# Sixteen words to an entry of the experts' lists, where there were four

## The chip, the cores and the metric

The kernel runs on one core of a Trainium2 chip. The metric is the device time of one execution in microseconds. Three runs of the kernel before were timed.

## The reference

An attention block with a decaying outer-product state makes x, and a top-2 mixture of eight experts works on it.

```python
# attention: B=4, H=8, S=768, D=48
f = sigmoid(f_logit)
for t in range(S):
    state = f[:, :, t, :, None] * state + einsum('bhd,bhe->bhde', k[:, :, t], v[:, :, t])
    y[:, :, t] = einsum('bhd,bhde->bhe', q[:, :, t], state)
x = y.transpose(0, 2, 1, 3).reshape(3072, 384)
# router and experts: E=8, F=1024
noisy = x @ w_gate + log1p(exp(x @ w_noise)) * noise          # (3072, 8)
top2, weights = the two largest of noisy, softmax over the two
for e in range(8):
    for k in range(2):
        m = top2[:, k] == e
        out[m] += weights[m, k, None] * (relu(x[m] @ w1[e]) @ w2[e])
```

## The kernel before, in words

**Attention.** The 3,072 tokens are 24 tiles of 128 (six chunks of the sequence times four batches). Tile n passes seven stages, `forget`, `scaled`, `scores`, `summed`, `output`, `decays`, `features`, and one loop (L1243) issues them for several tiles at once, each stage at its own lag. The inputs f, q, k, v of a tile are four loads of 128 x 8 pieces of 192 bytes, written into rings of 5, 4, 4 and 6 tiles (L424); `load` (L517) puts them on SP's queue in the order of the program, some tiles ahead. `clamp` (L523) works on f, from the second loop step on on POOL. A tile's x goes out to a DRAM table `x_rows` (L631).

**Routing.** After the four tiles of a chunk, `route` (L634) computes the noisy logits, the two experts of each token with their weights, and each token's rank among those of its expert. Its steps are spread over the stages of the next tiles. Its result is `entry` (L475): for each tile and each of the two choices an entry of four words, the row of x, the weight, the token, and a zero. `put` (L700) is one indirect DMA from POOL that writes the 128 entries of a tile and choice to their places in the DRAM table `lists` (L468), where each expert has 3,072 places. There are 48 puts; they are popped one by one between the stages (L1274), and each is followed by a small memset of `spacer`.

**Fill.** Places that no token takes must name a row that exists and a token that is out of bounds. `empty` (L469) holds such entries; four memsets at L1192 write it at the start, and one DMA (L1267, on SP's queue while tile 5 passes `scores`) copies it over all of `lists`. `entry` is cleared and gets its constant words at L1194 to L1196.

**Experts.** An item is a block of 256 places of one expert's list, or two such blocks. `fetch` (L795) loads 256 entries from `lists` into `slots` (SP's queue), `gather` (L806) collects the rows of x by indirect DMA from POOL, `turned` (L822) transposes them into `xt`, and `first_layer` (L872) or `first_of_two` (L891) and `second_layer` (L970) run the two matrix products. The result rows `ys` are scattered with add into `out` (L995). The first items use tokens of the first three chunks alone, so that they begin while attention still runs; further items take blocks of pairs with fewer products, and rests of 32 places go through `fetch_quarter` (L1073) and `quarter_block` (L1092). Behind two flags (L1336) stand code for further rests and a general version; neither is taken here.

**Memory.** SBUF tiles are placed in the order in which the pools and their tiles are made: `top`, `ring`, `moved`, `const`, `rt`, `ffn`, and behind these the attention's working tiles, later replaced by `late`. `empty` and `entry` are in `const`; `xt` and `hs` are in `ffn` and `late`; the expert weights `w1`, `w2` and the gathered rows are in `moved`, ahead of `const`.

The order of instructions on each engine is that of the program from L1199 on (`in_order`). DMAs issued from SP wait there, in order, for their buffers.

Of the kernel before, what the change touches and what calls it, by code (L numbers as in the profile page):

```python
# [12 lines left out]
U32 = mybir.dt.uint32  # L13
# [318 lines left out]
def kernel(  # L332
# [38 lines left out]
    nc = tc.nc  # L371
    B, H, S, D = q.shape
    N, DM = out.shape
    E = moe_w_gate.shape[1]
    FF = moe_w1.shape[2]
    C = 128
    NCH = S // C
# [5 lines left out]
    QS = 32  # L383
# [5 lines left out]
    FAR = 1 << 20  # L389
# [13 lines left out]
    const = ctx.enter_context(tc.tile_pool(name="const", bufs=1))  # L403
# [59 lines left out]
                            pattern=[[1, 128]], channel_multiplier=-1)  # L463


    LR = E * N + 256
    x_rows = tc.dram_tile([N, DM], F32, name="x_rows")
    lists = tc.dram_tile([LR, 4], U32, name="lists")  # L468
    empty = const.tile([128, LR // 128, 4], U32, tag="empty", name="empty")  # L469

    cap = [const.tile([128, HP, C], F32, tag=f"cap{i}", name=f"cap{i}") for i in range(2)]
    for i in range(2):
        nc.gpsimd.memset(cap[i], LCAP)

    entry = const.tile([128, NCH, B, 2, 4], U32, tag="entry", name="entry")  # L475


    XW = 2 * D
# [44 lines left out]
    def clamp(n, engine=nc.gpsimd):  # L523
        if n < NCH * B:
            raw = pads["f"][n % RING["f"]][:, :, 0:D]
            engine.tensor_scalar(raw, raw, XMIN, None, ALU.max)  # L526
# [241 lines left out]
    def value(at, hi):  # L768
        return nc.values_load(at, engines=[mybir.EngineType.SP], min_val=0, max_val=hi,
                              skip_runtime_bounds_check_because="clamped where it is made")  # L770

    slots, xg, xt = {}, {}, {}
# [13 lines left out]
    def item_of(p):  # L786
        return p if p < E else E + (p - E) // 2

    def expert_of(k):
        return k if k < E else NI - 1 - k  # L790
# [4 lines left out]
    def fetch(p):  # L795

        assert len(n_put) >= (HALF if p < E else NCH) * B * 2
        slots[p] = ffn.tile([128, 2, 4], U32, tag=f"slots{p < E}", name=f"slots{p}", bufs=8)
        row = expert_of(item_of(p)) * N + (0 if p < E else 256 * (1 + (p - E) % 2))
        got = nc.sync.dma_start(out=slots[p], in_=lists[row:row + 256, :].rearrange("(s p) w -> p s w", p=128))  # L800
        if p < E:

            tc.declare_no_dep(got.ins, group="later", reason="slots differ")
            tc.add_to_no_dep_group("full", got.ins)
# [265 lines left out]
    slots_q, xg_q = {}, {}  # L1070
    late, w_q = [], []

    def fetch_quarter(n):  # L1073

        slots_q[n] = ffn.tile([128, 4], U32, tag="slots_q", name=f"slots_q{n}", bufs=2)
        row = value(steer_q[n][:, 1:2], E * N)
        for i in range(128 // QS):
            nc.sync.dma_start(out=slots_q[n][i * QS:(i + 1) * QS, :], in_=lists[bass.ds(row, QS), :])

    def gather_quarter(n):  # L1080
        xg_q[n] = late[-1].tile([QS, DM], F32, tag="xg_q", name=f"xg_q{n}", bufs=2)
# [48 lines left out]
    def further(inner, steers):  # L1130

        sb = inner.enter_context(tc.tile_pool(name="sb", bufs=1))
        ps = inner.enter_context(tc.tile_pool(name="ps", bufs=2, space=PSUM))
        same = sb.tile([128, 128], F32, tag="same", name="same")
        make_identity(nc, same)
        for t, (steer, skip, size) in enumerate(steers):
            at, x = sb.tile([128, 4], U32, tag="at", name=f"at{t}"), sb.tile([128, DM], F32, tag="x", name=f"x{t}")
            if size < 128:
                for i, val in enumerate((0, 0, FAR, 0)):
                    nc.vector.memset(at[:, i:i + 1], val)  # L1140
            nc.sync.dma_start(out=at[0:size], in_=lists[skip:][bass.ds(value(steer[:, 1:2], E * N), size), :])
            nc.gpsimd.indirect_dma_start(out=x, out_offset=None, in_=x_rows,
                                         in_offset=bass.IndirectOffsetOnAxis(ap=at[:, 0:1], axis=0))
            e = value(steer[:, 0:1], E - 1)
            w1, w2 = sb.tile([128, KO, FF], F32, tag="w1", name=f"w1{t}"), sb.tile([128, FO, DM], F32, tag="w2", name=f"w2{t}")
            nc.sync.dma_start(out=w1, in_=moe_w1[bass.ds(e, 1)].rearrange("o (k p) f -> p (o k) f", p=128))
            nc.sync.dma_start(out=w2, in_=moe_w2[bass.ds(e, 1)].rearrange("o (f p) d -> p (o f) d", p=128))
            p = ps.tile([128, 512], F32, tag="p", name=f"px{t}")
            for i in range(KO):
                nc.tensor.transpose(p[:, i * 128:(i + 1) * 128], x[:, i * 128:(i + 1) * 128], same)  # L1150
            turn = sb.tile([128, KO, 128], F32, tag="turn", name=f"turn{t}")
            nc.vector.tensor_copy(turn.rearrange("d k t -> d (k t)"), p[:, 0:DM])
            h = sb.tile([128, FO, 128], F32, tag="h", name=f"h{t}")
            for fo in range(FO):
                p = ps.tile([128, 512], F32, tag="p", name=f"ph{t}_{fo}")
                for i in range(KO):
                    nc.tensor.matmul(p[:, 0:128], lhsT=w1[:, i, fo * 128:(fo + 1) * 128], rhs=turn[:, i, :],
                                     start=(i == 0), stop=(i == KO - 1))
                nc.scalar.activation(h[:, fo, :], p[:, 0:128], AF.Relu)
            p = ps.tile([128, 512], F32, tag="p", name=f"py{t}")  # L1160
            for fo in range(FO):
                nc.tensor.matmul(p[:, 0:DM], lhsT=h[:, fo, :], rhs=w2[:, fo, :], start=(fo == 0), stop=(fo == FO - 1))
            y = sb.tile([128, DM], F32, tag="y", name=f"yf{t}")
            nc.vector.tensor_scalar(y, p[:, 0:DM], at[:, 1:2].bitcast(F32), None, ALU.mult)
            nc.gpsimd.indirect_dma_start(out=out, out_offset=bass.IndirectOffsetOnAxis(ap=at[:, 2:3], axis=0),
                                         in_=y, in_offset=None, bounds_check=N - 1, oob_is_err=False, compute_op=ALU.add)
# [22 lines left out]
        nc.vector.tensor_tensor(rest, more, bad, ALU.max)  # L1189

    zero = moved.tile([128, DM], F32, tag="zero", name="zero", bufs=1)
    for i, val in enumerate((0, 0, FAR, 0)):  # L1192
        nc.gpsimd.memset(empty[:, :, i], val)
    nc.gpsimd.memset(entry, 0)  # L1194
    for i, ids in ((0, row_of), (2, token)):
        nc.gpsimd.tensor_copy(entry[:, :, :, :, i], ids.unsqueeze(3).broadcast_to((128, NCH, B, 2)))  # L1196
# [46 lines left out]
    for i in range(-3, NS + 2):  # L1243
        for stage, lag in ((forget, -3), (scaled, -1), (scores, 0), (summed, -2), (output, 1), (decays, -2), (features, 2)):
            n = i - lag
            if not 0 <= n < NS:
                continue
            stage(n)
            if stage is forget:
                load("f", n + 4)  # L1250
                clamp(n + 2, nc.gpsimd if n else nc.vector)
            elif stage is scaled:
                for nm in "qk":
                    load(nm, n + 2) if n < 4 else load(nm, n + 3)
                    if n == 3:
                        load(nm, n + 3)
                if n < 2:
                    load_router(n)
                while xw:
                    xw.pop(0)()  # L1260
            elif stage is scores:
                for m in (n + 1,) if n < 4 else (2 * n - 3, 2 * n - 2) if n < 6 else (n + 3,):
                    load("v", m)
                if n in (2, 6, 7, 8, 9, 10):
                    load_router(2 + (2, 6, 7, 8, 9, 10).index(n))
                elif n == 5:
                    nc.sync.dma_start(out=lists.rearrange("(p r) w -> p r w", p=128), in_=empty)  # L1267
            elif stage is output:
                if 5 <= n < 5 + NS // 2:
                    zeros(1)  # L1270
            next(router, None)
            slot += 1
            if puts and (slot % 3 == 0 or n_routed >= HALF):
                puts.pop(0)()  # L1274
            next(first_pairs, None)

            if done["turned"] and (n_first < 5 or i >= NS - 3 and stage is not forget) and (n_first < 11 or i >= NS - 1):
                next(pieces)
                n_first += 1
        if i < 0:  # L1280
            warm_up(4)
        if i >= NS - 1:
            while xw:
                xw.pop(0)()
        n = i - 2
        if n >= 0 and n % B == B - 1:
            c = n // B
            router = chain(router, route(c))
            n_routed = c + 1
            if c == HALF - 1:  # L1290
                router = chain(router, enough())
                first_pairs = first_loads()
            if c == NCH - 1:
                router = chain(router, plan(), beyond())
# [16 lines left out]
    for item, piece in pieces:  # L1311
        p = item if item < E else 2 * item - E + (piece >= 15)
# [4 lines left out]
        n = item - E - 2  # L1317
# [52 lines left out]
```

## Time and profile before

| | |
|---|---|
| median of three timed runs | 663.89 us (662.24 to 664.91) |
| profiled execution, its own time | 658.81 us |
| its span | 656.5 us |
| TensorE busy | 640.0 us, 97% |
| VectorE, ScalarE, POOL busy | 445.2, 249.7, 269.2 us |
| DMA | 108.90 MB, mean 166 GB/s, 157,161 packets |

The span is the profiled stretch of one execution; the own time has what lies around it. PE is TensorE, PEld its weight loads, DVE VectorE, ACT ScalarE, POOL GpSimd, SP SyncE, which here issues DMAs; SPq is SP's queue. L702 is line 702 of the kernel. A group's line gives the line, the engine, the operation, the tile written and those read, a count and durations. A wait's line names the engine that waited, its tile and line, and behind the arrow what it waited for; then microseconds in total, times, and the longest. "DMA share" is the mean busy share of the core's 16 DMA engines.

### The profile page before, as it was taken

To read this page: it belongs to the slowest core of one execution; us is meant where nothing else is said; L and a number is where in the kernel's file an instruction comes from. 1 tells how busy PE (TensorE), PEld (TensorE's weight loads), DVE (VectorE), ACT (ScalarE), POOL (GpSimd) and SP (SyncE) were. 2 spreads that over 40 slices of the span, in tenths; PEclk is the share of its full clock that TensorE was granted. 3 is DMA by queue.
4 is the path that set the end of the run, shared out by engine and by line. 5 is a ranking of instruction groups with operands and counts; after the bars stand their busy time and mean duration, and the time that the engine had idled before them with its cause. 6 is when DMAs were issued, how large, how long until landed. Compare 5 with 4: busy or idle time off the path is not lost.

```text
span 656.5 us, 13307 instructions
## 1 busy us (share of the span) xinstructions
PE 640.0 (97%) x5075; PEld 586.6 (89%) x5075; DVE 445.2 (68%) x1017; ACT 249.7 (38%) x611; POOL 269.2 (41%) x300
## 2 busy tenths in 40 slices
PE   8999999999999999999999999999999999999991
PEld 8999999888999999999999998998989989889891
DVE  7777878884667445544777767776676777766751
ACT  5876876743221221222333423333233333332320
POOL 7734899828476333212405033150341513413021
PEclk9999999999999999999999999999999999999997
DMA  9999997898799856532325485672954738602122
GB/s 178 183 220 200 205 196 126 179 299 286 225 216 257 263 171 205 174 103 49 73 97 119 121 270 163 228 203 72 303 169 166 211 110 306 183 2 25 22 25 29
DMA packets 157161, 108.90 MB, mean 166 GB/s; under 512 B 115536, under 2 KB 147280, under 8 KB 157088
## 3 DMA queue, kind: packets, MB, share of 16 engines
q1 hardware_dynamic: 144912, 88.70, 49.1%
q0 software_dynamic: 12176, 19.25, 14.0%
q8 instruction: 42, 0.69, 0.5%
q14 instruction: 31, 0.25, 0.1%
HBM read 88.56 MB, written 19.62 MB: 165 GB/s over the span
## 4 chain that ended last, share of the span: by engine, by line
PE 85%; POOL 8%; DVE 2%; DMA 2%; issue 1%; ACT 0%; POOLq 0%; DVEq 0%
PE y L986 32%; PE hp L878 13%; PE P L905 7%; PE Z L905 4%; PE V L905 4%; PE X L905 4%; PE W L905 4%; POOL lists L702 4%; PE xgp L827 2%; PE y L590 2%; PE xp L625 2%; PE sc L572 2%; POOL f_all L526 2%; PE yp_q L1120 1%; PE hp_q L1105 1%
## 5 line engine op out<-in xcount | busy, mean ns | idle before, releaser
L995 POOL DMA_INDIRECT out_dram<-ys,slots x48 | 80.4, 1675 | 198.3 <-ACT ys L1052 169.7
L986 PE MATMUL y<-qk_all,f_all 128*128 128x192 f32 x576 | 105.3, 326 | 0.0
L986 PEld LDWEIGHTS y<-qk_all,f_all 128*128 128x128 f32 x576 | 93.6, 190 | 0.2 <-DVE f_all L968 0.2
L878 PE MATMUL hp<-xt,w 128*128 128x256 f32 x384 | 86.2, 381 | 0.0
L878 PEld LDWEIGHTS hp<-xt,w 128*128 128x128 f32 x384 | 72.0, 190 | 9.6 <-issue 0.3
L986 PE MATMUL y<-w,hs 128*128 128x192 f32 x384 | 70.8, 327 | 0.0
L986 PEld LDWEIGHTS y<-w,hs 128*128 128x128 f32 x384 | 63.7, 190 | 1.2
L968 DVE TENSOR_TENSOR f_all<-hs 128x512 f32<-128x512 f32 x48 | 32.4, 689 | 41.9 <-ACT hs L880 36.5
L810 POOL DMA_INDIRECT xg<-x_rows,slots x48 | 50.2, 1046 | 25.9 <-DMA slots<-lists 11.9
L702 POOL DMA_INDIRECT lists<-entry,sloti x48 | 54.8, 1142 | 9.9 <-issue 9.3
L880 ACT ACTIVATE hs<-hp 128x512 f32<-128x512 f32 x32 | 19.1, 597 | 70.7 <-PE hp L878 70.7
L1126 POOL DMA_INDIRECT out_dram<-ys_q,slots_q x5 | 8.6, 1715 | 80.4 <-DVE ys_q L1124 80.4
L1052 ACT ACTIVATE ys<-ys,slots 128x384 f32<-128x384 f32 x24 | 14.8, 615 | 66.6 <-DVE ys L1051 64.7
L905 PE MATMUL P<-sides,v_all 128*128 128x256 f32 x128 | 38.1, 379 | 0.0
L828 ACT COPY xt<-xgp 128x384 f32<-128x384 f32 x32 | 15.3, 477 | 56.7 <-PE xgp L827 56.7
L941 ACT ACTIVATE hs<-hs 128x256 f32<-128x256 f32 x32 | 13.4, 418 | 59.4 <-DVE hs L921 59.4
L986 PE MATMUL y<-qk_all,hs 128*128 128x192 f32 x192 | 35.1, 326 | 0.0
L986 PE MATMUL y<-w,f_all 128*128 128x192 f32 x192 | 35.1, 326 | 0.0
L575 DVE TENSOR_TENSOR A<-sc,causal 128x1024 f32<-128x1024 f32 x24 | 29.3, 1221 | 7.7 <-PE sc L572 7.4
L905 PE MATMUL X<-xt,w 128*128 128x256 f32 x128 | 32.9, 379 | 0.0
L905 PE MATMUL Z<-xt,v_all 128*128 128x256 f32 x128 | 32.9, 379 | 0.0
L1044 DVE TENSOR_TENSOR ys<-P,y 128x192 f32<-128x192 f32 x24 | 8.5, 354 | 34.6 <-PE y L986 19.8
(189 smaller groups left out, 1385.8 us busy)
## 6 DMA issues: line engine op xcount, KB each, us to landing
w<-in_moe_w_dram SPq DMA_DIRECT2D x28, 1536.0 KB
w_q<-in_moe_w_dram SPq DMA_DIRECT2D x10, 1536.0 KB
f_all<-in_f_logit_dram SPq DMA_DIRECT2D x24, 192.0 KB
qk_all<-in_q_dram SPq DMA_DIRECT2D x24, 192.0 KB
qk_all<-in_k_dram SPq DMA_DIRECT2D x24, 192.0 KB
v_all<-in_v_dram SPq DMA_DIRECT2D x24, 192.0 KB
x_rows<-xs SPq DMA_DIRECT2D x24, 192.0 KB
out_dram<-zero SPq DMA_DIRECT2D x24, 192.0 KB
```

The source lines that it names most:

```text
L575: nc.vector.tensor_tensor(A[n].rearrange("j r (a i) -> j (r a) i", i=C), sc.rearrange("j r (a i) -> j (r a) i", i=C), causal.unsqueeze(1). ...
L702: into = nc.gpsimd.indirect_dma_start(out=lists, out_offset=bass.IndirectOffsetOnAxis(ap=sloti[:, r, b:b + 1], axis=0), in_=entry[:, c, b, ...
L810: nc.gpsimd.indirect_dma_start(out=xg[p][:, s, :], out_offset=None, in_=x_rows[0:HALF * B * C] if p < E else x_rows, in_offset=bass.Indire ...
L828: (nc.vector.tensor_copy if p < E else nc.scalar.copy)(xt[p][:, :, s * 128:(s + 1) * 128], xp[:, 0:DM].rearrange("d (k t) -> d k t", k=KO))
L878: nc.tensor.matmul(hp[:, o, :], lhsT=w1[home(k)][:, i, (fo + o) * 128:(fo + o + 1) * 128], rhs=xt[k][:, i, :], start=(i == 0), stop=(i == ...
L880: nc.scalar.activation(hs[:, fo:fo + 2, :], hp, AF.Relu)
L905: nc.tensor.matmul(to, lhsT=x, rhs=y, start=start, stop=stop)
L941: nc.scalar.activation(c(1, 1), c(1, 1), AF.Relu)
L968: nc.vector.tensor_tensor(sm[which], x, y, op)
L986: nc.tensor.matmul(P[name], lhsT=x[:, o, :], rhs=y[:, o, :], start=(o == 0), stop=(o == FH - 1))
L995: into = nc.gpsimd.indirect_dma_start(out=out, out_offset=bass.IndirectOffsetOnAxis(ap=slots[p][:, s, 2:3], axis=0), in_=ys[s], in_offset= ...
L1052: nc.scalar.mul(ys[1], ys[1], gate[1])
```

## The change

An entry has 16 words in `lists` and in `entry` instead of four; the twelve words behind the first four are zero and are never read. A put writes all 16. The readers take the first four words of each row. `lists` has 25,088 rows instead of 24,832. `empty` holds a quarter of the rows and is written by two memsets, one over all of it and one over the token word; four DMAs copy it, two while tile 3 passes `scores`, one at tile 4 and one at tile 5.

```diff
-    LR = E * N + 256
+    LR = E * N + 512
+    LW = 16
     x_rows = tc.dram_tile([N, DM], F32, name="x_rows")
-    lists = tc.dram_tile([LR, 4], U32, name="lists")
-    empty = const.tile([128, LR // 128, 4], U32, tag="empty", name="empty")
+    lists = tc.dram_tile([LR, LW], U32, name="lists")
+    empty = const.tile([128, LR // 128 // 4, LW], U32, tag="empty", name="empty")
...
-    entry = const.tile([128, NCH, B, 2, 4], U32, tag="entry", name="entry")
+    entry = const.tile([128, NCH, B, 2, LW], U32, tag="entry", name="entry")
...
-        got = nc.sync.dma_start(out=slots[p], in_=lists[row:row + 256, :].rearrange("(s p) w -> p s w", p=128))
+        got = nc.sync.dma_start(out=slots[p], in_=lists[row:row + 256, 0:4].rearrange("(s p) w -> p s w", p=128))
...
-            nc.sync.dma_start(out=slots_q[n][i * QS:(i + 1) * QS, :], in_=lists[bass.ds(row, QS), :])
+            nc.sync.dma_start(out=slots_q[n][i * QS:(i + 1) * QS, :], in_=lists[bass.ds(row, QS), 0:4])
...
-    for i, val in enumerate((0, 0, FAR, 0)):
-        nc.gpsimd.memset(empty[:, :, i], val)
+    nc.gpsimd.memset(empty, 0)
+    nc.gpsimd.memset(empty[:, :, 2], FAR)
     nc.gpsimd.memset(entry, 0)
...
-                elif n == 5:
-                    nc.sync.dma_start(out=lists.rearrange("(p r) w -> p r w", p=128), in_=empty)
+                elif 3 <= n < 6:
+                    for m in (0, 1) if n == 3 else (n - 2,):
+                        nc.sync.dma_start(out=lists.rearrange("(g p r) w -> g p r w", g=4, p=128)[m], in_=empty)
```

More of the change, by code (lines that the diff above doesn't have):

```diff
@@ L1140, in further @@
                     nc.vector.memset(at[:, i:i + 1], val)
-            nc.sync.dma_start(out=at[0:size], in_=lists[skip:][bass.ds(value(steer[:, 1:2], E * N), size), :])
+            nc.sync.dma_start(out=at[0:size], in_=lists[skip:][bass.ds(value(steer[:, 1:2], E * N), size), 0:4])
             nc.gpsimd.indirect_dma_start(out=x, out_offset=None, in_=x_rows,
```

## The prediction

> **What bounds the kernel now.** I read the page first, then the busy time by stretches, then the waits of TensorE, then the list's own groups, and last the packets and the start.
>
> ```profile
> span 656.5 us, 13307 instructions
> PE 640.0 (97%) x5075; PEld 586.6 (89%) x5075; DVE 445.2 (68%) x1017; ACT 249.7 (38%) x611; POOL 269.2 (41%) x300
> PE 85%; POOL 8%; DVE 2%; DMA 2%; issue 1%; ACT 0%; POOLq 0%; DVEq 0%
> ```
>
> TensorE has 640.0 of 656.5 us. Of the chain that ended last 85% is TensorE; the 8% on POOL are mostly stretches in which TensorE was busy too. So what matters is where the other 16.5 us are. The stretches tell (us from:to; busy us of PE, PEld, DVE, ACT, POOL with counts; granted clock; DMA share; GB/s):
>
> ```profile
> 0.00:66.00 66.00, 63.77 (x808) 58.70 (x808) 50.12 (x99) 47.67 (x120) 36.10 (x65) 1.00 0.94 196
> 66.00:130.00 64.00, 64.00 (x917) 58.24 (x917) 53.01 (x134) 46.12 (x126) 57.98 (x78) 1.00 0.87 178
> 130.00:150.00 20.00, 19.17 (x248) 16.37 (x246) 16.46 (x36) 9.62 (x27) 6.77 (x8) 1.00 0.98 285
> 150.00:216.00 66.00, 66.00 (x416) 61.32 (x411) 39.51 (x121) 15.90 (x35) 43.57 (x61) 1.00 0.90 246
> 216.00:643.00 427.00, 427.00 (x2701) 392.00 (x2699) 285.70 (x629) 130.39 (x306) 122.25 (x90) 1.00 0.51 146
> 643.00:656.50 13.50, 0.03 (x1) 0.00 (x0) 0.42 (x1) 0.00 (x0) 2.50 (x2) 0.66 0.28 34
> ```
>
> TensorE is idle 2.23 us up to 66, nearly all before the first tile is through, 0.83 us at the hand-over from attention to experts (130 to 150), and 13.47 us at the end, where the last scatters and the flags run. The change touches nothing after 643. It can win at most the 0.83 us and some tenths of the start; for more, runs without the profiler must hold stalls that this one lacks. TensorE's waits are all of it:
>
> ```profile
> PE warm L1207 <- DVE ones L435: 1.1, 1, 1.1
> PE fp L532 <- DVE f_all L526: 0.7, 1, 0.7
> PE xgp L827 <- ACT yT L605: 0.7, 1, 0.7
> PE qp L532 <- DMA qk_all<-in_q_dram: 0.2, 1, 0.2
> ```
>
> **What the lists cost now.** From the group of the lists:
>
> ```profile
> L702 POOL DMA_INDIRECT lists<-entry,sloti x48: 954/990/1931, 68.3 to 209.1; - x48
> L1267 SPq DMA_DIRECT2D lists<-empty x1: 920/920/920, 45.5 to 45.5; - x1
> DMA to landing us min/median/max: 4.9/6.5/10.4
> ```
>
> A put costs POOL 0.99 us for 128 rows of 16 bytes; a gather of 128 rows of 1,536 bytes has a median of 1.01 us (the group of xg). POOL's price does not follow the bytes: four times the bytes, no change. The packet records show a put as 16 packets of 128 bytes at 15 ns (median): 768 packets, 0.7 us spread over 16 engines. But other packets get stuck beside them: in slices of 4 us the longest 192-byte load packet is 0.2 to 0.9 us from 20 to 68, before the puts, and 2.0, 1.4 and 1.8 us in the three slices from 100 to 112, where the median is still 15 ns. DMA falls behind there:
>
> ```profile
> 66.00:96.00 30.00, 30.00 (x443) 27.45 (x441) 23.64 (x57) 22.35 (x62) 26.98 (x36) 1.00 0.92 197
> 96.00:116.00 20.00, 20.00 (x288) 18.25 (x281) 17.47 (x46) 14.16 (x38) 18.37 (x25) 1.00 0.77 139
> ```
>
> Counting packets in the order of issue (1,024 of 192 bytes to a load), a load of q, k or f mostly drains in 0.9 to 1.4 us before the puts (at most 2.0), and in 2.0 to 2.7 us from 97 to 111. The lead of a k tile over its transpose falls from 10.3 us at tile 16 to 3.85 us at tile 20 and is 5.6 at tile 23. It never reaches zero, so TensorE pays nothing. Whole 64-byte writes may cure this; the cure meets no wait of TensorE.
>
> **The change part by part.**
>
> Start, on POOL. Out go four memsets of 194 strided words (468 ns each, 1.87 us) and one of 192 words (0.31): 2.18. In come memsets of 784 and 768 words and one of 49 strided words. From the 128-word memset (204 ns) to the 512-word one (514 ns) a word costs 0.81 ns: 0.73 + 0.72; at the dearer rate of the 192-word one (1.62 ns a word) 1.27 + 1.25. The small one lies between 0.13 (32 words) and 0.47. In all 1.58 to 2.99 us, so -0.6 to +0.8; I take -0.2, as the flat memset of 448 words (461 ns) lies on the cheap rate. Behind them POOL waits 0.88 us for the tile of its first clamp at 8.41, which hides either end. The one leak is DVE: its first clamp, beside busy POOL, takes 1.05 us, its third, with POOL idle, 0.36. A clamp more or less under a memset is +0.7 or -0.7; I take 0.
>
> The fill, on SP's queue and DMA. One fill of 388 KB was 128 packets of 3,104 bytes at 122 ns: 1.04 us of 16 engines, drained in 1.5 us. Now there are four of 392 KiB: 3.1 us of DMA work more, 4.6 at the drained pace, and three more issues of some 0.9 us on SP. Two stand ahead of f tile 11, one ahead of f tile 12, the last where the old one was. Queued behind them on SP are the loads, the stores of x_rows and the noise. The leads: v tile 5 lands at 40.7 and is used at 45.1, 4.4 us, against two fills (2.1 to 3.1): 1.3 left. f tiles 11 to 14 have 6.2 to 7.2 over their clamps, against 3.1 to 4.6: 1.6 left. q and k have 9.4 and more. Four loads (1,024 packets of 15 ns on 16 engines, 0.96 us) and two stores (128 of 65 ns, 0.52 us) need 4.9 us of DMA in each 6.0 us step, so the lag is worked off at about 1.1 us a step, before the puts begin at 68. Nothing on TensorE: 0. If the cover were gone, each us of lag is a us.
>
> The puts. A packet of 512 bytes lies between the 192-byte one (15 ns) and the 1,536-byte one (65): 27 ns, 0.6 us of DMA more in all. The two ends: puts that stick the others no longer (the 0.83 us of the hand-over go), or twice as much (the 3.85 us lead is gone and TensorE waits some 2 us). The first gathers drain at 143.5 and TensorE starts on them at 143.69, so that stretch is tight. I take -0.4, half of the idle time: the long packets stand beside the puts, which speaks for the first end, but the wait at 143.69 is put down to ScalarE, not to the gather.
>
> [...] The stuck packets show a stall, not its cause; no row separates 16 from 64 bytes.
>
> The reads. `slots` and `slots_q` still fetch 16 bytes a row, now 64 apart: the trace's 6,784 packets of 16 bytes at 9 ns stay. The fetch at 218.10 that waited 3.1 us for the last put is followed on SP by a weight load at 225.22 that waits for TensorE. 0.
>
> SBUF. `empty` grows by 32 bytes a partition and `entry` by 2,304: all tiles made later (route, expert inputs, hidden rows, attention work) move by 2,336 bytes, 36.5 times 64. Rows on this: `sloti` and `slot` are 32-byte tiles in two copies 32 bytes apart, and their six casts take 171 to 179 ns; the eight `slots` copies are 32 bytes apart and the 24 scalings at L1034 take 454 to 456. So 0 by the nearest rows, but these are small operands on other engines than TensorE.
>
> Sum: 658.8 (656.5 span and 2.3 around it) - 0.4 = 658.4. The median of the timed runs, 663.9, lies 5.1 above the profiled execution; with the same gap that is 663.5.
>
> **The rivals.**
>
> Faster, 659: the runs of 662.2 to 664.9 are 3.4 to 6.1 us longer than the profiled one. If that is TensorE waiting for loads or first gathers, at leads of 3.9 and 0.2 us, whole writes give it back: 663.9 - 5 = 658.9. For it: the stuck packets, the tight hand-over. Against: this trace shows no such wait, and the gap may lie outside of the kernel's waits.
>
> Slower, 671, by layout: 1,088 matmul passes read `xt` or `sides` as moving operand (384 at L878, 704 at L905), now off a 64-byte line. If each costs one more read of 8 words at its own pace (12 passes of 256 words in 2.59 us, 216 ns each, so 6.7 ns), that is 7.3 us: 671.2. It decides if reads do not run ahead; half of it is still slower by 0.5%. Against: the casts and scalings above.
>
> Slower, 668, by the fills: if four fills cost more than the 4.4 us lead (say 2.2 us each, as loads did among puts), v tile 5 and the f tiles come late and the stalls, up to 4 us, are not regained, as TensorE has no idle time to give.
>
> That whole lines are not what unsticks the engines is the forecast with its -0.4 left out: 663.9.
>
> **How the numbers follow.** No change that counts 0.45, faster by freed DMA 0.25, layout 0.18, fills 0.12. About 0.5% (3.3 us) is what a measurement of this kernel can tell from none: faster 0.25, same 0.45, slower 0.30. Likeliest 663.5, its own range 661.5 to 665.5. The 8-in-10 range reaches to the rivals' prices: 658.5 to 671.0.
>
> **What would show it.** TensorE near 640 us busy and packed from 15 to 643; v tile 5 landed before 45 us; DMA share above 0.85 between 96 and 116 with no 192-byte packet over 1 us if whole writes unstick the engines; L878 at 381 ns and L986 at 326 if layout is nothing. A wait of TensorE on a load between 32 and 70 us, or longer matmuls at L878, would prove me wrong.

## The result, and the profile after

The first comparison put the changed kernel at 671.40 us (four runs, 667.83 to 673.57) and the kernel before at 663.21 (four runs, 662.24 to 664.91): ratio 1.0115, 95% interval 1.0066 to 1.0165. The prediction was 663.5 with a range up to 671.0, so this is 7.9 us slower than predicted and above the top of the range. (Times are medians; a ratio and its interval come from the single runs and need not be the ratio of the medians. Five runs of before that lie over 1.5% above its fastest on their occasion are left out of the ratios: 1,266, 1,342 and 3,770 us beside the second timing of after, 673.27 us beside the fifth, and 680.42 us beside the last timing of pitch only.) The same kernel, timed again on other occasions (an occasion is the runs of one comparison, taken on one chip one after the other), was no slower than before: 658.36 against 658.67, 658.49 against 658.81, 657.85 against 658.70. On a further occasion it was slower again: 670.69 against 663.81, ratio 1.0106 (1.0055 to 1.0157). What follows is about both halves of that: why the change is worth nothing where the machine is undisturbed, and what is known of the other occasions, on which before itself needs 662 us and more.

The page of the profiled execution after (671.40 us), whose span and busy times answer to those of before:

```profile
span 669.3 us, 13308 instructions
...
PE 645.6 (96%) x5075; PEld 589.7 (88%) x5075; DVE 442.3 (66%) x1017; ACT 250.0 (37%) x611; POOL 262.3 (39%) x298
...
PEclk9999999997999999999999999999999999999996
```

TensorE is busy 5.6 us longer and idle 7.2 us longer (669.3 - 645.6 = 23.7, before 16.5). One slice of the clock row reads 7: the granted clock fell to a half for 6.8 us from 153.7 us on. The same stretches as before (from:to; length, then busy us of PE, PEld, DVE, ACT, POOL; clock; DMA share; GB/s):

```profile
0.00:66.00 66.00, 63.78 (x804) 58.74 (x804) 49.33 (x98) 47.30 (x118) 35.81 (x63) 1.00 0.96 207
66.00:130.00 64.00, 62.77 (x876) 55.99 (x870) 48.23 (x128) 44.82 (x120) 52.09 (x76) 1.00 0.87 199
130.00:150.00 20.00, 19.57 (x270) 16.95 (x265) 14.92 (x28) 9.83 (x28) 12.89 (x17) 1.00 0.88 276
150.00:216.00 66.00, 59.83 (x372) 54.07 (x371) 35.89 (x112) 15.23 (x34) 27.51 (x39) 0.95 0.66 212
216.00:655.00 439.00, 438.95 (x2771) 403.54 (x2771) 293.50 (x653) 132.75 (x311) 130.90 (x104) 1.00 0.51 146
```

TensorE is idle no longer than before up to 66 us (63.78 busy against 63.77), where the four fills run, and not after 216. All the new idle time but that of the end (13.6 us against 13.5) lies between: 1.23 us idle from 66 to 130, where before had none, and 6.17 from 150 to 216. The waits of TensorE say what for:

```profile
PE hp L879 <- issue: 6.0, 1, 6.0
...
PE sc L573 <- issue: 0.8, 4, 0.2
```

"issue" is a wait that this view puts down to nothing: no load, no gather, no other engine. (The timelines say more about the 6.0 us; they are read under "What the occasion does".) The put is as cheap as expected, 48 at 0.98 us (median; before 0.99). The issues of the four fills took SP 1.35 us (median) where 0.9 was expected, and 0.96 and 1.09 in the second and third profile of after:

```profile
L703 POOL DMA_INDIRECT lists<-entry,sloti x48: 954/982/2002, 68.9 to 223.6; - x48
...
L1269 SPq DMA_DIRECT2D lists<-empty x4: 1009/1348/1594, 33.7 to 48.0; - x4
```

### The profile page after: what moved, and what is told of

It reads as the page before. It is cut to its first block, busy times and chain, and to the rows that moved or that the text cites. A ratio compares the mean times of both kernels' runs of the same rounds, so it can differ in the third digit from the quotient of the medians.

```text
span 669.3 us, 13308 instructions
## 1 busy us (share of the span) xinstructions
PE 645.6 (96%) x5075; PEld 589.7 (88%) x5075; DVE 442.3 (66%) x1017; ACT 250.0 (37%) x611; POOL 262.3 (39%) x298
## 4 chain that ended last, share of the span: by engine, by line
PE 93%; issue 2%; DVE 1%; DMA 1%; ACT 1%; POOL 0%; POOLq 0%; DVEq 0%
PE y L987 31%; PE hp L879 13%; PE P L906 6%; PE Z L906 4%; PE V L906 4%; PE X L906 4%; PE W L906 4%; PE sc L573 4%; PE xp L626 4%; PE y L591 4%; PE xgp L828 2%; PE y L602 2%; PE fp L533 2%; PE qp L533 2%; PE ds L597 1%
## 5 line engine op out<-in xcount | busy, mean ns | idle before, releaser
L987 PE MATMUL y<-qk_all,f_all 128*128 128x192 f32 x576 | 105.2, 326 | 0.0
L879 PE MATMUL hp<-xt,w 128*128 128x256 f32 x384 | 87.9, 386 | 6.1 <-issue 6.0
L987 PEld LDWEIGHTS y<-qk_all,f_all 128*128 128x128 f32 x576 | 93.6, 190 | 0.2 <-DVE f_all L969 0.2
L879 PEld LDWEIGHTS hp<-xt,w 128*128 128x128 f32 x384 | 73.2, 193 | 16.5 <-issue 6.6
L987 PE MATMUL y<-w,hs 128*128 128x192 f32 x384 | 70.8, 327 | 0.0
L987 PEld LDWEIGHTS y<-w,hs 128*128 128x128 f32 x384 | 63.7, 190 | 1.2
L811 POOL DMA_INDIRECT xg<-x_rows,slots x48 | 50.6, 1055 | 17.9 <-issue 10.4
L703 POOL DMA_INDIRECT lists<-entry,sloti x48 | 51.8, 1079 | 9.9 <-issue 9.6
L906 PE MATMUL P<-sides,v_all 128*128 128x256 f32 x128 | 38.1, 379 | 0.0
L987 PE MATMUL y<-qk_all,hs 128*128 128x192 f32 x192 | 35.1, 326 | 0.0
L987 PE MATMUL y<-w,f_all 128*128 128x192 f32 x192 | 35.1, 326 | 0.0
L906 PE MATMUL X<-xt,w 128*128 128x256 f32 x128 | 32.8, 379 | 0.0
L906 PE MATMUL Z<-xt,v_all 128*128 128x256 f32 x128 | 32.8, 379 | 0.0
```

What stands on the lines that cost most here:

```text
L703: into = nc.gpsimd.indirect_dma_start(out=lists, out_offset=bass.IndirectOffsetOnAxis(ap=sloti[:, r, b:b + 1], axis=0), in_=entry[:, c, b, ...
L811: nc.gpsimd.indirect_dma_start(out=xg[p][:, s, :], out_offset=None, in_=x_rows[0:HALF * B * C] if p < E else x_rows, in_offset=bass.Indire ...
L879: nc.tensor.matmul(hp[:, o, :], lhsT=w1[home(k)][:, i, (fo + o) * 128:(fo + o + 1) * 128], rhs=xt[k][:, i, :], start=(i == 0), stop=(i == ...
L906: nc.tensor.matmul(to, lhsT=x, rhs=y, start=start, stop=stop)
L987: nc.tensor.matmul(P[name], lhsT=x[:, o, :], rhs=y[:, o, :], start=(o == 0), stop=(o == FH - 1))
```

## The experiments

Two theories at first: one of the parts (whole writes, fills, layout) costs some 8 us, or none does and the first comparison met something else. Four kernels put the parts one by one.

Pitch only: a put writes 16 bytes at a pitch of 64.

```diff
-        nc.vector.tensor_copy(sloti, slot)
+        nc.vector.tensor_scalar(sloti, slot, float(LW // 4), None, ALU.mult)
...
-                out=lists, out_offset=bass.IndirectOffsetOnAxis(ap=sloti[:, r, b:b + 1], axis=0),
-                in_=entry[:, c, b, r, :], in_offset=None)
+                out=lists.rearrange("l (a w) -> (l a) w", w=4), out_offset=bass.IndirectOffsetOnAxis(ap=sloti[:, r, b:b + 1], axis=0),
+                in_=entry[:, c, b, r, 0:4], in_offset=None)
```

> After, but a put writes only the first 16 bytes of its 64-byte row; rows, fills and layout stay as in after. Theory 'whole writes' (the 64-byte writes themselves, or the loads that they let run ahead, cause the 10 us lost between 98 and 161 us): 663 to 665 us, the longest 192-byte packets between 96 and 116 us back near 2 us, the wait of TensorE before the first hp matmuls under 1 us. Rival 'fills': 671. Rival 'layout': 671.

Small fill:

```diff
-                elif 3 <= n < 6:
-                    for m in (0, 1) if n == 3 else (n - 2,):
-                        nc.sync.dma_start(out=lists.rearrange("(g p r) w -> g p r w", g=4, p=128)[m], in_=empty)
+                elif n == 5:
+                    for e in range(E):
+                        nc.sync.dma_start(out=lists[e * N + 512:e * N + 1024, :].rearrange("(p r) w -> p r w", p=16), in_=empty[16 * e:16 * e + 16, 0:32])
+                    nc.sync.dma_start(out=lists[E * N:LR, :].rearrange("(p r) w -> p r w", p=128), in_=empty[:, 0:4])
```

> After, with one fill of 288 KB (the rows 512 to 1023 of each expert and the 512 of the tail, in nine transfers at step 5) in place of four of 392 KB; the rows that no block reads are not filled. Theory 'whole writes': 671 us, the wait of some 6 us before the first hp matmuls stays. Rival 'fills' (three more transfers shift the loads): 663 to 665. Rival 'layout': 671.

Before with room, and before with three unused fills:

```diff
     entry = const.tile([128, NCH, B, 2, 4], U32, tag="entry", name="entry")
+    const.tile([128, 584], U32, tag="room", name="room")
```

> Before, with an unused tile of 2,336 bytes a partition behind the entries: every later tile lies where it lies in after. Theory 'whole writes': 663 to 665 us. Rival 'layout': 671, with a wait before the first hp matmuls. Rival 'fills': 663 to 665.

```diff
+    dummy = tc.dram_tile([3, 128, 784], U32, name="dummy")
+    full = const.tile([128, 784], U32, tag="full", name="full")
...
-                elif n == 5:
-                    nc.sync.dma_start(out=lists.rearrange("(p r) w -> p r w", p=128), in_=empty)
+                elif 3 <= n < 6:
+                    for m in (0, 1) if n == 3 else (n - 2,):
+                        if m < 3:
+                            nc.sync.dma_start(out=dummy[m], in_=full)
+                        else:
+                            nc.sync.dma_start(out=lists.rearrange("(p r) w -> p r w", p=128), in_=empty)
```

> Before, with three transfers of 392 KB from an unused tile to an unused tensor where after has its three more fills. Theory 'whole writes': 663 to 665 us. Rival 'fills': 670 to 672, with a wait before the first hp matmuls. Rival 'layout': this kernel moves tiles by 3,136 bytes, 49 lines of 64 bytes, so 663 to 665 by it.

Measured, beside a before of 658.58 us (31 runs): 658.49 (ratio 0.9997, 0.9984 to 1.0009), 657.91 (0.9991, 0.998 to 1.0001), 658.18 (1.0002, 0.999 to 1.0013) and 658.38 (1.0002, 0.9993 to 1.0012). No part costs 0.2% here. (Pitch only was also expected to bring the long packets back; its longest 192-byte packet took 0.65 us, which is taken up below.) But before is also 4.6 us faster than in the first comparison, so the parts had not yet been tried under the condition in which the whole lost. The whole was, next.

> After, unchanged, timed anew. Pitch-only puts, the small fill, the layout and the dummy fills each ran within 0.1% of before (658.6 us there). Theory 'interaction' (whole writes and four fills cost only together): 668 to 672 us while before is at 658 to 659, with some 6 us of TensorE wait before the first hp matmuls. Rival 'occasion' (the first comparison, where before itself ran at 662 to 665 us, met a disturbance that neither kernel makes, and after only had less margin against it): 658 to 659 us beside a before of 658.6, TensorE's completion events never more than 2.9 us apart before 230 us, and the first hp matmuls at 146 to 147 us; or, where before runs at 662 to 665 again, after above it again.

> Pitch-only puts again, beside after on the same chip. Theory 'interaction': 658 to 659 us, at least 1.5% under after. Rival 'occasion': the same as after where before is at 658.6; where before runs at 662 to 665, both above before, by up to 8 us.

After 658.36 and pitch only 658.18 beside a before of 658.67 (ratios 1.0004, 0.9995 to 1.0013, and 0.9993, 0.9982 to 1.0004). The theory of an interaction falls: parts and whole are alike, and none differs from before by 0.2%. The same program thus has spans of 656.0 and 669.3 us. So the occasion decides, and the question splits: does the change do anything, and what does the occasion do?

**What the change does.** The prediction left open whether whole writes free the loads that stick beside puts. The next runs asked what it is in the rows that frees them, and whether that is worth time once DMA is pressed.

> After, unchanged, a third time (the second time it ran at 658.4 beside a before of 658.7). Theory 'occasion': 658 to 659 us and ratio 0.998 to 1.002 where before is at 658 to 659; only where before itself is at 662 or above, 668 or more. Rival 'real loss of 1%': 665 us or more beside a before of 658.7.

> After with entries of 32 bytes in place of 64 (two fills in place of four). Theory 'pitch' (the nearer the rows of concurrent puts lie, the longer other packets stick beside them): the longest 192-byte packet lies between the 0.65 to 0.85 us of the 64-byte kernels and the 1.2 to 1.3 us of those with 16; the sum of all 192-byte packets between 95.7 and 97.8 us. Rival 'only whole 64-byte lines are clean': 1.2 us and 97.8 again. Time by both: 658 to 659 us.

After ran at 658.49 against 658.81 (0.9991, 0.998 to 1.0002), entries of 32 bytes at 658.56 (1.0003, 0.9991 to 1.0014). From the packet records, over all profiles of each kind without extra copies (long: 192-byte load packets of over 0.6 us that start between 66 and 212 us, while the puts run; sum: the packet time of all 98,304 load packets over 16 engines; the last column is over the whole run):

| rows of the lists | kernels | long | sum, us | longest weight packet (4,096 bytes), us |
|---|---|---|---|---|
| pitch 16, write 16 | before (two profiles), room, unused fills (two) | 14 to 42 | 97.6 to 101.4 | 1.9 to 3.0 |
| pitch 32, write 32 | entries of 32 bytes | 1 | 95.1 | 1.2 |
| pitch 64, write 16 | pitch only (four) | 0 to 4 | 95.4 to 95.6 | 1.1 to 1.4 |
| pitch 64, write 64 | after (five), small fill | 0 to 2 | 95.1 to 96.1 | 1.1 to 1.4 |

Writing all 64 bytes is not what frees the loads: 16 bytes written at a pitch of 64 do it as well (0 to 4 long packets), and so do 32 at 32 (one). Of the pitches tried only 16 bytes makes other packets stick (14 to 42). That it would go by degrees, with 95.7 to 97.8 us for rows of 32 bytes, did not come true: 95.1 is as clean as 64. The table does not show the cause.

Is it worth time? The same ten extra copies went into before and into after:

```diff
...
                 if 5 <= n < 5 + NS // 2:
                     zeros(1)
+                if 12 <= n < 22:
+                    nc.sync.dma_start(out=extra[n - 12], in_=moe_w1[0, 0:96, :])
```

> Before, with one extra copy of 384 KB from DRAM to DRAM on SP's queue in each of the ten steps 12 to 21 (some 2.1 us of 16 engines each, beside 4.9 us of loads and stores in a step of 6.0). Theory 'headroom' (the 64-byte pitch lets the loads run ahead, which is worth time only where DMA is the bound): the lead of 3.85 us is eaten, TensorE waits for loads, 661 to 668 us. Rival 'dense DMA itself delays TensorE's completions': 665 us or more, with completion events more than 3 us apart. If DMA has more to give than that: 658.6.

> After, with the same ten copies. Theory 'headroom': the lead of 15 us at tile 20 covers the copies, 658 to 660 us, 2 to 8 us under before with the copies. Rival 'dense DMA itself delays completions': as slow as before with the copies, or slower.

Before goes to 661.17 us (1.0052, 1.0026 to 1.0077, against 658.81), after stays at 658.53 (0.9994, 0.9984 to 1.0003). A copy took 1.2 us of 16 engines, less than expected. The waits of TensorE from start to end, first of before with the copies, then of after with them:

```profile
PE xgp L828 <- DMA xg<-x_rows,slots: 1.4, 1, 1.4
PE warm L1208 <- DVE ones L435: 1.1, 1, 1.1
```

```profile
PE warm L1209 <- DVE ones L435: 1.1, 1, 1.1
PE fp L534 <- DVE f_all L528: 1.0, 1, 1.0
```

In after the third longest is 0.3 us, and none is for DMA. In before the copies come out as 1.4 us of waiting for the first gather at the hand-over; the smallest lead of a k tile (tiles 14 to 23) is 4.3 us there, 9.1 in after. The single runs of before with the copies spread from 659.07 to 666.01 us, and the profiled one took 660.53. So the changed rows buy headroom of DMA, and without extra traffic there is nobody to spend it. That it is their pitch is argued from the table; pitch only did not run with the copies. The lead alone does not tell the kernels apart: at tile 20 it is 9.0 us in one profile of pitch only. The same pair from one chip, with no copies:

> Before itself, profiled beside its own timed runs: the null of the comparison, and a profile from the same chip as the next run. 658 to 659 us, ratio within 0.2% of 1, if this chip is like the last three. Theory 'pitch' (16-byte rows make other packets stick, 32 and 64-byte rows don't): the longest 192-byte packet 1.2 us or more, all of them 97.8 to 101 us of packet time. Rival 'the stuck packets of the first profile belonged to that occasion': under 0.9 us and 96. If the chip is one where before needs 662 to 665: a wait or late completion events near the hand-over at 140 to 150 us.

> After beside it. Theory 'occasion': the same as before within 0.2% where before runs at 658 to 659; 5 to 9 us above it where before runs at 662 to 665. Rival 'real loss': 665 us or more either way. The longest 192-byte packet under 1.1 us, 95 to 96 us in all.

Before against itself: 658.92 to 658.70 (0.9998, 0.9985 to 1.0011). After: 657.85 (0.9987, 0.9978 to 0.9997), the only one of the twelve undisturbed intervals without copies that leaves 1 out, by 0.03%; one in twelve at 95% is little more than chance gives. Before again has 14 long packets, the longest 1.9 us, so they belong to the kernel and not to the first profile's occasion. The DMA rows from 96 to 116 us, before again and then after:

```profile
96.00:116.00 20.00, 20.00 (x302) 18.14 (x298) 18.07 (x47) 13.41 (x35) 18.20 (x26) 1.00 0.92 194
...
130.00:150.00 20.00, 18.80 (x240) 16.14 (x239) 17.66 (x36) 9.55 (x26) 11.29 (x16) 1.00 0.94 295
```

```profile
96.00:116.00 20.00, 20.00 (x293) 18.20 (x290) 17.77 (x46) 13.84 (x37) 18.34 (x25) 1.00 0.95 223
...
130.00:150.00 20.00, 19.84 (x258) 16.92 (x260) 17.27 (x37) 10.04 (x27) 13.82 (x19) 1.00 1.06 366
```

At nearly the same share of DMA time, 223 GB/s come through instead of 194. Divided by the share, this stretch has 181 to 212 GB/s in the five profiles with rows 16 bytes apart and 227 to 235 in the eight undisturbed ones with rows 32 or 64 apart, none of them with copies. TensorE is full from 96 to 116 either way; at the hand-over it is idle 0.16 us instead of 1.20. With rows 16 bytes apart that number varies (0.83 in the first profile, 1.49 with room, 0.16 and 0.63 with unused fills); in the other eight it is 0.15 to 0.17.

**What the occasion does.** Then an occasion like the first came up, for after alone and for both kernels with the copies doubled:

```diff
-                    nc.sync.dma_start(out=extra[n - 12], in_=moe_w1[0, 0:96, :])
+                    for m in (0, 1):
+                        nc.sync.dma_start(out=extra[2 * (n - 12) + m], in_=moe_w1[m, 0:96, :])
```

> After, unchanged, beside another set of runs of before. Theory 'occasion': 657.5 to 659 us and 0.1% at most from before. Rival 'real loss': 665 us or more.

> Before with two extra copies of 384 KB in each of the ten steps 12 to 21. One copy took 1.2 us of 16 engines, so a step of 6.0 us now needs 4.9 + 2.4 = 7.3, and ten steps fall 13 us behind against leads of 8 to 13 us. Theory 'headroom': TensorE waits for loads or for the first gathers, 662 to 672 us. If the copies only fill DMA's idle time after the loads: 661 as with one copy.

> After with the same copies. Theory 'headroom': leads of 10 to 16 us cover most of it, 658 to 663 us, at least 2 us under before with the same copies. Rival 'after has less margin at the hand-over': above before with the same copies, TensorE waiting before the first hp matmuls.

Beside a before of 663.81 us: after 670.69 (1.0106, 1.0055 to 1.0157), before with two copies a step 687.78 (1.0373, 1.0301 to 1.0445), after with them 670.44 (1.0094, 1.0063 to 1.0126). Both kernels with copies took longer than expected (662 to 672, and 658 to 663 us). On this occasion after alone is 6.9 us slower than before; with the copies the order turns round, and the changed kernel is 17.3 us faster. TensorE's longest waits, first of before and then of after with double copies:

```profile
PE qp L533 <- DMA qk_all<-in_q_dram: 6.7, 5, 2.4
PE xgp L828 <- DMA xg<-x_rows,slots: 4.2, 1, 4.2
PE kp L533 <- DMA qk_all<-in_k_dram: 3.3, 4, 1.4
```

```profile
PE xgp L829 <- DMA xg<-x_rows,slots: 2.3, 1, 2.3
PE y L592 <- issue: 1.7, 2, 1.1
```

And copies of 22 us of 16 engines leave the time of after where it was on that occasion (670.44 against 670.69), so a denser DMA by itself does not make its loss larger. What it loses is seen when two of the five profiles of after are laid side by side, the third (undisturbed) and the fifth (disturbed). The third:

```profile
150.00:165.00 15.00, 15.00 (x124) 13.17 (x121) 4.43 (x16) 4.32 (x11) 4.17 (x8) 1.00 0.55 192
```

and the fifth:

```profile
150.00:165.00 15.00, 12.42 (x63) 8.84 (x64) 3.57 (x9) 1.63 (x4) 6.36 (x12) 0.77 0.57 202
```

From 150 to 165 us half as many matmuls start. The timeline of TensorE (start, us, engine, line, count, and in brackets the idle time before it) shows how, in the third run and then in the fifth:

```profile
150.11 0.67 PE L602 MATMUL y<-qP,st 64*64 64x128 f32 x16
150.71 1.56 PE L879 MATMUL hp<-xt,w 128*128 128x256 f32 x6
```

```profile
153.75 0.45 PE L602 MATMUL y<-qP,st 64*64 64x128 f32 x8
154.43 0.31 PE L602 MATMUL y<-qP,st 64*64 64x128 f32 x1 [0.23 <-issue]
155.15 0.27 PE L602 MATMUL y<-qP,st 64*64 64x128 f32 x1 [0.41 <-issue]
155.86 0.42 PE L602 MATMUL y<-qP,st 64*64 64x128 f32 x2 [0.44 <-issue]
157.28 1.07 PE L602 MATMUL y<-qP,st 64*64 64x128 f32 x3 [1.00 <-issue]
158.72 0.44 PE L602 MATMUL y<-qP,st 64*64 64x128 f32 x1 [0.37 <-issue]
```

Sixteen matmuls of one product, with no wait for another engine or a load in the trace, start within 0.67 us in the one and take 5.4 us in the other, the late ones at steps of 0.71 us or twice that. From 157.4 us on, before the product is through, the granted clock is a half for 6.8 us. Of the 11.5 us between the two spans 3.6 are lost before 150 us, 4.8 in this product, 2.5 in the hp passes behind it, which run at half clock, and 0.6 later.

In the first run of after the 6.0 us look different. From its timelines of TensorE and VectorE:

```profile
148.95 0.49 PE L828 MATMUL xgp<-ident,xg 128*128 128x128 f32 x3
156.46 0.56 DVE L829 COPY xt<-xgp 128x384 f32<-128x384 f32 x1 [0.58 <-remote]
157.08 4.11 PE L879 MATMUL hp<-xt,w 128*128 128x256 f32 x10 [6.02 <-issue]
```

("remote" stands for a releaser that the profile does not name.) The matmuls of hp read xt, and they start 0.06 us behind the copy that makes it. So here TensorE did wait for another engine. The copy in turn began 7.0 us after the product xgp that it reads was done; in the third run the same two steps are 0.4 us apart, with DVE still busy in between. What DVE waits for is the increment of a semaphore by which TensorE reports. From 147.7 to 151.1 us six products end whose increments come 2.2, 3.0, 3.9, 5.9, 7.0 and 7.0 us later (in the third run 0.02 us), and in each case the copy or operation on ScalarE or VectorE that waits for it starts 0.02 to 0.03 us behind the increment. The ends of matmuls are modelled in these profiles, so it stays open whether the matmuls or their reports were late. The increments come 0.75, 1.42, 2.86, 1.43 and 1.58 us apart, near multiples of the 0.71 us of the fifth run.

Both runs of after on such occasions show this from 75 to 225 us, and in the same stretch their traces miss records: 1,797 and 1,822 increments of the semaphores, against 3,027 to 3,129 in the other three. Every profile of an undisturbed occasion has 8,541 to 8,729 of these records in all, the first profile of before among them (8,557), every one of the disturbed ones 6,968 to 7,614, the kernels with double copies at the upper end.

The lost records and the pauses fall in the same 150 us; no run here shows that the one makes the other, and before itself was never profiled on such an occasion. One explanation, code that reaches TensorE late, finds no support: from 75 to 225 us the third and the fifth run each have 19 packets in the queues that the page calls instruction, with a median of 0.93 and 0.95 us.

Which part of the change loses more on such an occasion? Pitch only and unused fills once more:

> Pitch-only puts (16 bytes at a pitch of 64, four fills). On a chip where before needs 658 to 659 us: the same within 0.2%. On one where before needs 662 to 665: 669 to 672 if the pitch or the fills (loads and transfers bunched earlier) make the loss there, 662 to 665 if the 64-byte writes do.

> Before with three unused fills. On a chip where before needs 658 to 659 us: the same within 0.2%. On one where before needs 662 to 665: 669 to 672 if the fills or the shift of the tiles make the loss there, 662 to 666 if the puts' rows do, by their pitch or their bytes.

An undisturbed occasion: 658.05 and 658.87 against 658.61 (0.9985, 0.997 to 1.0001, and 0.9998, 0.9983 to 1.0014); it repeats the null and tells nothing of the others. And again:

> Pitch-only puts (16 bytes at a pitch of 64, four fills). On a chip where before needs 658 to 659 us: the same within 0.2%. On one where before needs 662 to 665: 669 to 672 if the pitch or the fills make the loss there, 662 to 665 if the 64-byte writes do.

This one was disturbed, more than the others: before 668.98 us (665.65 to 680.42), pitch only 674.61, ratio 1.0067 (1.0025 to 1.0109). It is the same program that had 658.05 an occasion earlier. Its timeline has the same picture at another product:

```profile
155.38 0.81 PE L573 MATMUL sc<-qP,kQ 64*128 64x128 f32 x4 [0.45 <-issue]
156.79 0.82 PE L573 MATMUL sc<-qP,kQ 64*128 64x128 f32 x4 [0.60 <-issue]
158.22 0.59 PE L573 MATMUL sc<-qP,kQ 64*128 64x128 f32 x2 [0.61 <-issue]
```

So the extra loss does not need 64-byte writes; it comes with 16 bytes at a pitch of 64, four fills and the moved tiles too. Pitch, fills and layout were not told apart under this condition: the runs meant for it met undisturbed occasions. The extra loss on disturbed occasions is measured (two intervals for after, one for pitch only, all above 1); its cause is open. The granted clock goes with it: beside the fifth run all four runs of after have a mean of 0.987 or 0.988, and 12 of the 13 of before 0.990 to 0.993; the one run of before at 0.987 took 673.27 us.

## Why the prediction was wrong, and where it was right

The step that failed is the last line of the sum: "with the same gap that is 663.5". The sum itself, 658.8 - 0.4 = 658.4, is what after takes on undisturbed occasions (658.36, 658.49, 657.85). The gap of 5.1 us between the profiled execution and the median was taken as a constant that any version would carry. In the comparison the gap was zero: the profiled execution of after took 671.40 us, which is also the median, and that is 13.0 above the sum. The gap of before was the mark of a disturbed occasion: by its complete records and its 658.81 us the profile of before came from an undisturbed execution, by their times the timed runs did not. What such an occasion adds is no constant either: from one kind of occasion to the other before took 5.2 us more (658.6 to 663.8), after 12.3 (658.4 to 670.7), and pitch only 16.6 (658.05 to 674.61, on the worst occasion, where before took 10.4 more). What the runs show in place of the gap is TensorE's pauses, late reports and half clock of the last section, which the prediction had nowhere. Before itself was not profiled there, and why after loses more than before stays open. The rival "faster" was the only place where the gap was looked at; it read it as waits for loads that freed DMA would return, and the sign was the opposite.

By its own steps, the rest:

- *What bounds the kernel.* Right: TensorE, busy for 97% of the span before and 96% in the first profile of after. (The list of its waits leaves out a fifth, 0.2 us for VectorE at L575.) Loads cost it little: none in the first, third, fourth and fifth profile, and in the second 0.6 and 0.4 us near 15 us and 0.5 us at 45. On an undisturbed occasion after has the hand-over at 19.84 of 20 us busy.
- *Start.* The three memsets took 0.74, 0.18 and 0.74 us, 1.66 in all, near the low end of 1.58 to 2.99. The leak by DVE is real: the first f transposes start at 5.10 us instead of 4.79 in every kernel with the changed memsets. The times do not show it.
- *The fill, 0.* Right in the time, with a thinner cover than reckoned. The 1.3 us that were to be left of the lead of v tile 5 were 1.9 to 4.3 us in four profiles of after (from the last landing to the use; by this measure before had 3.7). In the second profile, an undisturbed one, the last landing came at 45.16 us, and TensorE, which started on the tile at 45.30, had waited for it:

```profile
PE y L591 <- DMA v_all<-in_v_dram: 0.5, 1, 0.5
```

  Two experiments on fills lie within 0.1% of nothing, and that comparison has 658.36 against 658.67. The rival at 668 falls.
- *The puts, -0.4.* The packets of 512 bytes took 27 ns, as worked out. The stuck packets went, the k lead of after at tile 20 is 11.0 to 15.9 us, and the difference to before is -0.3, -0.3 and -0.9 us in the three undisturbed comparisons. That agrees with -0.4, but two of the three intervals do not tell it from 0, and 0.4 us was below what a measurement here can show. The reason is a neighbour of the stated one: the pitch frees the loads (0 to 4 long packets at 64, whether 16 or 64 bytes are written), not the write of all 64 bytes. What the trace of before did not tell is that its lead of 3.85 us was a low one; the other kernels with 16-byte rows and no copies have 7.6 to 11.4 there.
- *Layout, 0.* Right. L987 took 326 ns, L906 379, L879 381 on undisturbed occasions, as before, so the 6.7 ns a pass, the author's estimate, show nowhere, and the tile of 2,336 bytes alone gives 1.0002. The rival at 671 had the right number by the wrong way: in the first run L879 rose from 381 to 386 ns, through passes at half clock, 384 x 5 ns = 1.9 us, and the others of the experts kept their times.
- *What would prove it wrong.* Both signs that were named appeared in some profile, and neither is the failure. The wait for a load, 0.5 us at v tile 5, came in an undisturbed run; the longer matmuls at L879, 386 and 389 ns, came from the half clock (in the first run 631 ns a pass there, 379 behind it). The failure came by what was not named: TensorE's pauses and late reports on some occasions.

## What to carry to other kernels

If a profiled execution is some us faster than the timed runs, the gap is a term to be explained, not a constant to be added: take a second profile, on the occasion of the timed runs, before the medians are compared. Time the same program on several occasions before a difference of 1% is put down to an edit; here one program gave 658 and 675 us, and each comparison's interval held only for its own occasion. And what one engine is freed of can be worth nothing while another is full: here TensorE was busy for 97% of the span, and the freed DMA brought no time (658.49 against 658.81 us). Press the freed engine, as the copies did, to see what the headroom is worth (658.53 against 661.17).

## What the runs showed of the hardware

- In this kernel scatter rows of 16 bytes that lie 16 bytes apart hold up unrelated packets: while the puts ran, 14 to 42 load packets of 192 bytes took over 0.6 us (median 0.015), against 0 to 4 with rows 32 or 64 bytes apart, whether 16, 32 or 64 bytes of the row are written.
- On three of eight occasions the same programs took 5 to 17 us longer. The profiles taken there (all of changed kernels or of kernels with copies) miss some 14 to 19% of their semaphore records (6,968 against 8,570 for after; for those with double copies against 8,730 and what a second set adds), TensorE starts matmuls for which the trace shows no wait in steps of 0.71 us or twice that, and in the first run of after its increments came up to 7.0 us behind the modelled ends. The chip's number does not tell it: one number was undisturbed in one comparison and disturbed in another.
- About the pauses at the hand-over the granted clock is a half for 6.8 us in both disturbed runs of after: the first hp passes behind them came every 0.43 us instead of 0.22, and in the fifth run twelve of them took 2.4 us more.
